# Attention and a bilinear feed-forward layer on one core: turned weights read in four transfers, maxima kept in PSUM, signs ahead of shifts, and half of the first queries at first

## The chip, the core and the metric

The kernel runs on one core of a Trainium2 chip. Its engines are TensorE (PE, with its own weight loads, PEld), VectorE (DVE), ScalarE (ACT), GpSimd (POOL) and SyncE (SP), which here only issues DMAs. The metric is the device time of one execution in microseconds (us); lower is better. Three executions of the kernel before took 1405.77, 1406.40 and 1414.82 us, so the median is 1406.40. A further execution was profiled.

## The reference

```python
# 8 batches x 8 heads, 576 positions, 64 columns a head; tau = 0.02
scores = scale * np.matmul(q, k.transpose(0, 1, 3, 2))
thresh = np.max(scores, axis=-1, keepdims=True) - tau
scores = np.where(scores >= thresh, scores, -1000000000.0)
scores = scores - np.max(scores, axis=-1, keepdims=True)
attn = np.exp(scores)
attn = attn / (np.sum(attn, axis=-1, keepdims=True) + 1e-09)
out = np.matmul(attn, v)
# the heads side by side: x is 4608 tokens x 512
a = x @ w_a          # 512 x 1536
b = x @ w_b          # 512 x 1536
return a * b @ w_out # 1536 x 512
```

Only scores within tau of the row's maximum count in the softmax. The weights w_a, w_b and w_out come as 64-bit numbers, and the kernel turns them into 32-bit ones by operations on their bits.

## The kernel before

**Units and slots.** Heads are taken in pairs (32 pairs, numbered i; four of them make a batch). The 576 queries of a pair are four tiles of 128 (u = 0 to 3) and a tail of 64; the tails of two pairs make one more tile (u = 4). One such tile is a unit. The main loop (L1117) takes one unit per slot g; the instructions are written out in the order of the loop, and each engine runs its own in that order. The first four pairs' units 0 and 1 come first (slots 0 to 7), then their units 2, 3 and 4.

**What a slot does.** `scores` (L389) multiplies queries by keys on PE into two PSUM tiles (one for each head), and takes the maximum of each head on DVE (L411) and from both the threshold (L412). `weigh` (L422) makes a bias from the maximum (ACT, L431), the exponential (ACT, L432) and the product of mask and exponential with its sum (DVE, L435), tile `tw`. Sums become reciprocals (L446, L448). Then the weights `tw` must be turned, so that PE can multiply them by the values (products `pv`, L546):
- units of slots 0 to 7 are turned on PE (L483, with the division by the sum folded into a diagonal matrix, L462), and copied out by ACT (L485) and DVE (L486);
- later units are divided on ACT (L454), turned in blocks of 32x32 on DVE (L502, `turn_blocks`), written to memory (`swap<-tw`) and read back block by block in the other order (`wT<-swap`, `turn_back`, L517).

The result `xT` is copied out of PSUM by DVE (L554) and ACT (L553). The feed-forward layer follows behind: its first products are `pab` (L854, and L750 with seven products in place of eight), its last ones `po` (L920). `advance` (L1024) puts portions of it between the steps of a slot.

**Queries and keys.** Those of the first four pairs are loaded as rows (`load_rows`, L193), transposed by PE (L378, twelve 96x96 blocks for 576 rows of both heads) and copied out of PSUM: queries on DVE (`prep_copy`, L383) into `first_sb`, keys on ACT. Those of the other pairs are loaded in another layout and transposed by DVE (L365, `prep`): their queries in two halves, `q0` for units 0 and 1, `q1` for the others.

**Weights, while they are converted.** They come in 36 pieces of 512 columns, in two 32-bit words a number. Slots 0 to 3 start two pieces each, slots 4 to 9 three, slots 10 to 14 two; each piece is finished a slot later. A piece takes ACT twice (upper word L298, lower word L299), POOL (clamp, L305), DVE (sign into the lower word, L311, which reads two tiles of SBUF; then a shift of the upper word by three bits, L319) and POOL again (add, L324). `convert_rest(g, k)` does sign, shift and add of the piece k: piece 0 behind the threshold of the slot, pieces 1 and 2 at the end of the slot, with a step of `advance` between them in slots 0 to 8. During slots 0 to 15 `state["wide"]` is true; the scores then take 128 columns of queries at a time.

**Queues.** All loads, and writes and reads of `swap`, go through SP. From slot 37 on (`state["paced"]`) `post` (L139) puts moves in a list, and `passed` (L169) takes them off as PE's work goes by, by their sizes; each waits for the PE instruction behind which it was taken off (L157). `flush` empties the list up to what a product needs. Before slot 37 moves are issued at once (L144).

Of the kernel before, what the change touches and what calls it, by code (L numbers as in the profile page):

```python
# [10 lines left out]
FP32 = mybir.dt.float32  # L11
# [43 lines left out]
def kernel(  # L55
# [38 lines left out]
    nc = tc.nc  # L94
    B, H, S, D = q.shape
    P = 128
# [3 lines left out]
    HP = H // 2  # L100
# [5 lines left out]
    R = 96  # L106
    NR = S // R
    SH = S // 2
    NF = DFF // P
    HALF = MAIN // 2  # L110
    GT = HALF // TAIL
    NSLOT = 9
    G = P // Q
# [4 lines left out]
    def pool(name, bufs, **kw):  # L118
        return ctx.enter_context(tc.tile_pool(name=name, bufs=bufs, **kw))
# [4 lines left out]
    small = pool("small", 2)  # L124
    scratch = pool("scratch", 5, space=bass.MemoryType.DRAM)
    psum = pool("psum", 4, space=PSUM)

    def banks(n, name):

        return psum.tile([P, 2, 512], FP32, tag="banks", name=name)[:, :, 0:n]  # L130
# [3 lines left out]
    NPR = len(pairs)  # L134
# [4 lines left out]
    def post(key, *moves):  # L139

        if not state["paced"]:
            for move in moves:
                state["turn"] += state["over"]
                (nc.scalar if state["turn"] % 2 else nc.sync).dma_start(*move)  # L144
        else:
            at = len(bulk)
            if key[0] in ("tw", "wT"):
                while at and bulk[at - 1][0][0] not in ("tw", "wT") and bulk[at - 1][1] >= state["slot"] - 1:
                    at -= 1
            bulk.insert(at, (key, state["slot"], moves))  # L150
# [13 lines left out]
    def flush(*keys):  # L164

        while any(key in keys for key, _, _ in bulk):
            pump(1, False)
# [25 lines left out]
    def load_rows(i, name, room, engine=nc.sync):  # L193

        b, hp = pairs[i]
        for j in range(2):
            rows = {"q": q, "k": k}[name][b, 2 * hp + j]
            engine.dma_start(room[:, :, j * D:(j + 1) * D], rows.rearrange("(n p) d -> p n d", p=R))
        loaded.setdefault(i, {})[name] = room

    def load_v(i, again=False):
# [24 lines left out]
    for f in range(NG):  # L226
        for c in range(HP):
            for dst, w in ((wa_sb, w_a), (wb_sb, w_b)):
                src = []
                for r in range(2):  # L230
                    chunks = [(2 * c + e) % HP * 2 + (r + (c >= HP // 2)) % 2 for e in range(2)]
                    cols = slice(f * CW + r * CH, f * CW + (r + 1) * CH)
                    rows = w[:, cols].bitcast(U32).rearrange("(k p) f -> p k f", p=D)
                    src.append(rows[:, chunks[0]:chunks[1] + 1:2])
                pieces.append((dst[:, f, 2 * c:2 * c + 2].rearrange("p k f -> p (k f)"), src))
    for F in range(NF):
# [3 lines left out]
    state = {"loaded": 0, "added": 0, "converted": 0, "rows": 0, "sums": False, "through": 0, "over": False,  # L240
             "layer": False, "paced": False, "all": False, "turn": 0, "due": NPIECES, "wide": True, "slot": 0, "reading": False, "first": 0}
# [8 lines left out]
    first_sb = first_u32.bitcast(FP32)  # L250
# [57 lines left out]
    def convert_sign(n):  # L308
        if n in stages:
            low, hi = stages[n].bitcast(U32), raws.pop(n)[:, :, 1]  # L310
            nc.vector.scalar_tensor_tensor(out=low, in0=hi, scalar=0x80000000, in1=low,  # L311
                                           op0=ALU.bitwise_and, op1=ALU.bitwise_or)
            if n in taken:
                extra.append(taken.pop(n))

    def convert_shift(n):
        if n in stages:
            top = pieces[n][0].bitcast(U32)
            nc.vector.tensor_scalar(top, top, 3, None, op0=ALU.logical_shift_left)  # L319

    def convert_add(n):
        if n in stages:
            top, low = pieces[n][0].bitcast(I32), stages.pop(n).bitcast(I32)
            nc.gpsimd.tensor_tensor(top, top, low, op=ALU.add)  # L324
            state["added"] += 1
# [6 lines left out]
    for _ in range(TW_BUFS):  # L332
        t = work.tile([P, 2 * NB, Q], FP32, tag="tw", bufs=TW_BUFS, name="rows")
# [21 lines left out]
    prepared, scored, weights, turned, whole = {}, {}, {}, {}, {}  # L355
# [5 lines left out]
    def prep(i, name):  # L361

        flush((name, i))
        mT = loaded[i].pop(name).rearrange("p n e -> p (n e)")
        nc.vector.transpose(mT, mT)  # L365
        prepared.setdefault(i, {})[name] = mT

    def prep_pe(i, name):

        m = loaded[i][name]  # L370
        if name == "q":
            mT = first_sb[:, i * S:(i + 1) * S]
        else:
            mT = work.tile([P, S], FP32, tag="kT", bufs=HP, name="kT")
        tp = banks(SH, "tp")
        for c in range(2):
            for n in range(NR // 2):
                nc.tensor.transpose(tp[:, c, n * R:(n + 1) * R], m[:, c * (NR // 2) + n], ident[0:R, 0:R])  # L378
        prepared.setdefault(i, {})[name] = mT
        return mT, tp  # L380

    def prep_copy(mT, tp):
        nc.vector.tensor_copy(mT.rearrange("p (c k) -> p c k", c=2), tp)  # L383

    def columns():

        return P if state["wide"] else D

    def scores(i, u):  # L389
        qT, kT = prepared[i]["q" if i < HP else "q1" if u > 1 else "q0"], prepared[i]["k"]  # L390
        base = HALF if i >= HP and u > 1 else 0
        sc = [banks(SH, "sc") for _ in range(2)]
        wide = D if u == NT else columns()
        each = [(c, t, j) for c in range(2) for t in range(2 if wide == D else 1) for j in range(2)]
        if units.index((i, u)) < BY_HEAD:
            each.sort(key=lambda x: x[2])
        for c, t, j in each:
            r = slice(j * D, (j + 1) * D)
            if u < NT:
                m, o, q0 = j, t, u * P + t * D - base  # L400
            else:
                m, o, q0 = t, j ^ t, MAIN - base
                qT, kT = prepared[i + t]["q" if i < HP else "q1"], prepared[i + t]["k"]
            nc.tensor.matmul(sc[m][o * D:o * D + wide, c], qT[r, q0:q0 + wide],  # L404
                             kT[r, c * SH:(c + 1) * SH], start=True, stop=True)
        mx = small.tile([P, 2], FP32, tag="mx", name="mx")
        thr = small.tile([P, 2], FP32, tag="thr", name="thr")
        bias = small.tile([P, 2], FP32, tag="bias", name="bias")
        for j in range(2):
            c = slice(j, j + 1)  # L410
            nc.vector.tensor_reduce(mx[:, c], sc[j], axis=AX.XY, op=ALU.max)  # L411
        nc.vector.tensor_scalar(thr, mx, cut, None, op0=ALU.subtract)  # L412
        scored[i, u] = (sc, thr, bias, mx)
# [53 lines left out]
    def turned_tile(here=None):  # L467
        if here == (0, NT):
            return sums_sb[:, NSUM - TURNED:].rearrange("p (g s e) -> p g s e", g=G + 1, s=NSLOT)
        return work.tile([P, G + 1, NSLOT, Q], FP32, tag="wT", bufs=2, name="wT")  # L470
# [46 lines left out]
    def turn_back(i, u):  # L517

        key = "wT", i, min(u // 2, 1) if i >= HP else u // 2
        if u < NT or i < HP:  # L520
            flush(("tw", i, u))
            swap = swaps.pop((i, u)).rearrange("g p e -> p g e")
            turned[i, u] = turned_tile((i, u))
            for y in range(0, G, 2):
                post(key, (turned[i, u][:, y:y + 2].rearrange("p g s e -> p g (s e)"), swap[:, y:y + 2]))
        if i >= HP and u == (3 if i % 2 else NT):
            flush(("tw", i - i % 2, NT))
            swap = swaps[i - i % 2, NT].rearrange("g p e -> p g e")
            for y in range(2):
                post(key, (turned[i, 2 + y][:, G].rearrange("p s e -> p (s e)"), swap[:, i % 2 * 2 + y]))  # L530
            if i % 2:
                del swaps[i - 1, NT]
# [561 lines left out]
    kT, tp = prep_pe(0, "k")  # L1094
# [7 lines left out]
    nc.vector.tensor_tensor(cut, cut, big, op=ALU.add)  # L1102
    early = {}

    def convert_rest(g, k):

        for n in early.get(g - 1, [])[k:k + 1]:
            convert_sign(n)
            convert_shift(n)
            convert_add(n)  # L1110

    n = 0
    for g in range(NPIECES):
# [3 lines left out]
    for g in range(len(units) + PV_LAG):  # L1117
# [9 lines left out]
        if BY_PE + 1 < g <= len(units) + 1:  # L1127
            n = g - PV_LAG
# [3 lines left out]
        if here:  # L1132
            i, u = units[g]
# [10 lines left out]
            running["owed"] -= NSLOT * P // 2  # L1144
        if g < 3:
            prep_copy(*prep_pe(g + 1, "q"))
        convert_rest(g, 0)
        if g == 0:
            for c in range(0, 2 * QUARTER - 2 * CW + 1, 2 * CW):
                extra.append(more_u32[:, c:c + 2 * CW].rearrange("p (f w) -> p f w", w=2))  # L1150
# [7 lines left out]
        load_weights(RAWS if g < 9 else 3, most=1)  # L1158
        if here:
            weigh(i, u)  # L1160
        for p in range(HP, NPR):
            for name, d in (("q0", 1), ("q1", 1)):
                if g == (second if name == "q1" else first)[p] - d - (name == "q1" and p % 2):
                    prep(p, name)
        if here and g < BY_PE:
            reciprocal(i, u, nc.vector)
        if g < 3:
            kT, tp = prep_pe(g + 1, "k")
# [3 lines left out]
        if g > BY_PE:  # L1172
            n = g - PV_LAG
# [25 lines left out]
        elif here:  # L1199
            reciprocal(i, u, nc.scalar if converting else nc.vector)  # L1200
            normalise(i, u)
        convert_rest(g, 1)
        if g <= BY_PE:
            advance(pace)
        convert_rest(g, 2)
        for n in early.get(g, [])[1:]:
            convert_first(n)
            convert_clamp(n)
        load_weights(RAWS if g < 9 else 3, most=1)
        for p in range(HP, NPR):  # L1210
            for name, d in (("q0", 3), ("k", 4), ("q1", 3)):
                if g == (second if name == "q1" else first)[p] - d - (name == "q1" and p % 2):
                    load(p, name)
        for p in range(1, NPR):
# [67 lines left out]
```

## Time and profile before

| | |
|---|---|
| runs | 1405.77, 1406.40, 1414.82 us |
| profiled execution | 1400.57 us, span 1398.8 us, mean granted clock 0.998 |
| PE busy | 1361.5 us (97%) |
| DVE busy | 1013.9 us (72%) |
| ACT busy | 680.8 us (49%) |
| POOL busy | 492.8 us (35%) |
| DMA | 223.21 MB in 327449 packets, mean 160 GB/s |

The page of the profile cuts the span into 40 slices of 35 us. Each digit below is the busy share of a slice in tenths (9 is 90% or more); the last row is what the DMA engines moved.

```profile
PE   7889999999999999999999999999999999999998
DVE  6999877787777768786767776778777776745425
ACT  6977555545554555544454545454545455431110
GB/s 211 241 212 223 204 206 173 174 170 187 174 154 168 190 192 155 176 190 160 143 143 160 186 180 159 136 190 169 181 130 161 199 190 154 137 146 19 4 19 18
```

The transfers that the change touches, by kind (written and read tile, queue, count, size, median time from issue to landing):

```profile
wT<-swap SPq DMA_DIRECT2D x242, 288.0 KB, 3.8
...
wT<-swap SPq DMA_DIRECT2D x56, 144.0 KB, 3.6
qT<-in_q_dram SPq DMA_DIRECT2D x112, 40.0 KB, 2.8
...
rows<-in_q_dram SPq DMA_DIRECT2D x4, 144.0 KB, 4.3
sums_u<-in_q_dram SPq DMA_DIRECT2D x4, 144.0 KB, 6.4
```

The maximum of slot 0 starts at 10.2 us, that of slot 5 at 46.0, of slot 10 at 93.7 and of slot 16, the first one without weights to convert, at 141.3 us. ACT's copies of weights, biases and exponentials stand almost back to back from 30 to 73 us: it idles under 4 us there. In slots 0 to 15 the threshold took, in this order, 0.23, 0.23, 0.65, 0.38, 0.61, 0.60, 0.58, 0.60, 0.59, 0.23, 0.26, 0.58, 0.27, 0.60, 0.48 and 0.60 us. Later, SP issues 1055 transfers between 350 and 1250 us; that takes it 553 us, 0.38 us for a read of turned weights, and it waits for PE's places for most of the rest.

### The profile page before, as it was taken

What the parts mean: (1) busy time and instruction counts of PE and PEld (TensorE: products, weight loads), DVE (VectorE), ACT (ScalarE), POOL (GpSimd) and SP (SyncE); (2) the same over time, 40 slices, a digit from 0 to 9 for tenths busy, and PEclk for the clock granted to TensorE, in tenths of its full rate; (3) what the DMA queues carried; (4) which work ended last, traced back from release to release, by engine and by line L of the source; (5) the groups of instructions that cost most, each with busy time, mean ns of one, the idle gap of its engine ahead of it and who ended that gap; (6) DMA issues with size and microseconds to landing.
All of it is one profiled execution on the core that took longest, in us unless ns stands there. A gap on an engine that the chain in (4) does not pass through costs nothing.

```text
span 1398.8 us, 76307 instructions
## 1 busy us (share of the span) xinstructions
PE 1361.5 (97%) x33836; PEld 1258.5 (90%) x33836; DVE 1013.9 (72%) x2205; ACT 680.8 (49%) x1248; POOL 492.8 (35%) x675
## 2 busy tenths in 40 slices
PE   7889999999999999999999999999999999999998
PEld 5677588999998799999999999998899998799998
DVE  6999877787777768786767776778777776745425
ACT  6977555545554555544454545454545455431110
POOL 2764543424150607060515142332515060708100
PEclk9999999999999999999999999999999999999999
DMA  9977876667666775676556775566656775550000
GB/s 211 241 212 223 204 206 173 174 170 187 174 154 168 190 192 155 176 190 160 143 143 160 186 180 159 136 190 169 181 130 161 199 190 154 137 146 19 4 19 18
DMA packets 327449, 223.21 MB, mean 160 GB/s; under 512 B 171600, under 2 KB 311632, under 8 KB 327120
## 3 DMA queue, kind: packets, MB, share of 16 engines
q1 hardware_dynamic: 323936, 216.95, 60.1%
q8 instruction: 266, 4.36, 1.3%
q10 hardware_dynamic: 3184, 1.38, 0.4%
q14 instruction: 63, 0.52, 0.1%
HBM read 128.58 MB, written 89.65 MB: 156 GB/s over the span
## 4 chain that ended last, share of the span: by engine, by line
PE 88%; DMA 5%; DVE 4%; SPq 2%; issue 1%; ACT 1%; ACTq 0%; DVEq 0%
PE pab L750 29%; PE po L920 22%; PE pab L854 18%; PE sc L404 9%; PE pv L546 9%; SPq L144 1%; DMA vm<-in_v_dram 1%; DMA wT<-swap 1%; DVE tw L435 1%; DVE mx L411 1%; DMA more_u<-in_moe_w_a_dram 1%; DVE low L311 0%; DMA more_u<-in_moe_w_b_dram 0%; DVE tw L502 0%; DMA sums_u<-in_k_dram 0%
## 5 line engine op out<-in xcount | busy, mean ns | idle before, releaser
L454 ACT ACTIVATE tw<-tw,rcp 128x576 f32<-128x576 f32 x272 | 196.1, 768 | 201.3 <-DVE rcp L448 201.3
L411 DVE TENSOR_REDUCE mx<-sc 128x1 f32<-128x576 f32 x288 | 204.6, 752 | 121.2 <-PE sc L404 120.9
L432 ACT ACTIVATE tw<-sc,bias,scalars 128x576 f32<-128x576 f32 x288 | 239.6, 832 | 10.4 <-DMA qT<-in_q_dram 0.4
L712 POOL TENSOR_TENSOR h<-h,u 128x512 f32<-128x512 f32 x28 | 35.2, 1277 | 590.4 <-DVE h L824 414.1
L435 DVE SCALAR_TENSOR_TENSOR tw<-sc,thr,tw 128x576 f32<-128x576 f32 x288 | 220.9, 797 | 12.3 <-ACT tw L432 11.9
L920 PE MATMUL po<-wo_sb,h 64*64 64x256 f32 (+1 forms) x3408 | 210.5, 367 | 0.0
L502 DVE STREAM_TRANSPOSE tw<-tw 128x576 f32<-128x576 f32 x272 | 194.4, 752 | 0.8 <-ACT tw L454 0.8
L920 PEld LDWEIGHTS po<-wo_sb,h 64*64 64x64 f32 x3408 | 169.8, 133 | 14.9
L404 PE MATMUL sc<-kT,qT 64*64 64x288 f32 x2016 | 170.3, 404 | 1.8 <-issue 0.9
L546 PE MATMUL pv<-wT,vm 64*64 64x128 f32 (+2 forms) x4896 | 164.0, 275 | 3.7 <-DMA vm<-in_v_dram 1.4
L546 PEld LDWEIGHTS pv<-wT,vm 64*64 64x64 f32 x4896 | 153.2, 133 | 12.0 <-issue 4.0
L920 PE MATMUL po<-sums_u,h 64*64 64x256 f32 x2448 | 156.6, 376 | 0.0
L883 POOL TENSOR_TENSOR h<-h 128x256 f32<-128x256 f32 x168 | 117.2, 731 | 110.9 <-PE po L920 106.1
L750 PE MATMUL pab<-xU,wb_sb 64*64 64x128 f32 x4352 | 137.8, 269 | 0.0
L920 PEld LDWEIGHTS po<-sums_u,h 64*64 64x64 f32 x2448 | 126.1, 133 | 12.3 <-DVE h L862 0.5
L750 PEld LDWEIGHTS pab<-xU,wb_sb 64*64 64x64 f32 x4352 | 133.3, 133 | 1.8 <-ACT h L806 0.5
L404 PEld LDWEIGHTS sc<-kT,qT 64*64 64x64 f32 x2016 | 108.8, 133 | 17.3 <-issue 4.9
L431 ACT ACTIVATE bias<-mx,scalars 128x1 f32<-128x1 f32 x288 | 82.7, 287 | 66.1 <-DVE mx L411 65.6
L553 ACT COPY xT<-pv 128x128 f32<-128x128 f32 (+1 forms) x68 | 17.6, 259 | 193.5 <-PE pv L546 193.5
L750 PE MATMUL pab<-xS,wa_sb 64*64 64x128 f32 x2176 | 108.5, 269 | 0.8 <-issue 0.8
L554 DVE COPY xT<-pv 64x128 f32<-64x128 f32 (+1 forms) x136 | 38.1, 280 | 80.5 <-PE pv L546 79.0
L535 ACT COPY kept<-po 128x512 f32<-128x512 f32 x65 | 34.8, 535 | 120.3 <-PE po L920 106.4
(163 smaller groups left out, 2468.7 us busy)
## 6 DMA issues: line engine op xcount, KB each, us to landing
wT<-swap SPq DMA_DIRECT2D x242, 288.0 KB, 3.8
swap<-tw SPq DMA_DIRECT2D x480, 144.0 KB, 3.1
vm<-in_v_dram SPq DMA_DIRECT2D x128, 72.0 KB, 2.6
swap<-tw SPq DMA_DIRECT2D x128, 72.0 KB, 2.9
kT<-in_k_dram SPq DMA_DIRECT2D x112, 72.0 KB, 3.2
wT<-swap SPq DMA_DIRECT2D x56, 144.0 KB, 3.6
out_dram<-kept SPq DMA_DIRECT2D x27, 256.0 KB, 3.7
qT<-in_q_dram SPq DMA_DIRECT2D x112, 40.0 KB, 2.8
```

The costliest lines, as they stand in the source:

```text
L404: nc.tensor.matmul(sc[m][o * D:o * D + wide, c], qT[r, q0:q0 + wide], kT[r, c * SH:(c + 1) * SH], start=True, stop=True)
L411: nc.vector.tensor_reduce(mx[:, c], sc[j], axis=AX.XY, op=ALU.max)
L431: nc.scalar.activation(bias[:, j:j + 1], mx[:, j:j + 1], AF.Copy, scale=e_nscale)
L432: nc.scalar.activation(wb[j], sb[j], AF.Exp, bias=bias[:, j:j + 1], scale=e_scale)
L435: nc.vector.scalar_tensor_tensor(out=wv, in0=sb[j], scalar=thr[:, j:j + 1], in1=wv, op0=ALU.is_ge, op1=ALU.mult, accum_out=sums[:, j:j + 1])
L454: nc.scalar.activation(w, w, AF.Copy, scale=rcp[:, j:j + 1])
L502: nc.vector.transpose(w, w)
L546: nc.tensor.matmul(pv[c * D:(c + 1) * D, y], vm[rows, s], wT[y](rows, s), start=(s == 0), stop=(s == NSLOT - 1))
L750: nc.tensor.matmul(out[c * D:(c + 1) * D, r, f * P:(f + 1) * P], w[g][k][rows, w0:w0 + D], moving[k][rows], start=(fresh and k == 0 and f ...
L854: nc.tensor.matmul(pab[c:c + columns(), r], w[rows, f // n, k, fs + c:fs + c + columns()], moving, start=(k == 0), stop=(k == H - 1))
L883: (nc.vector if state["over"] else nc.gpsimd).tensor_tensor(*a, **kw)
L920: nc.tensor.matmul(po[c * D:(c + 1) * D, r, y, cut], ht[rows, t0:t0 + D], other[rows, f, cut], start=(f == 0), stop=(f == NF // 2 - 1))
```

## The change

Four edits:
1. The queries of the first four pairs are loaded, transposed and copied only up to row 288 (units 0 and 1 need 256). For units 2, 3 and 4 their second half comes as `q1`, as with the other pairs: 16 loads of 40 KB, and four transposes on DVE.
2. While weights are converted, the two maxima go to two free columns of the first head's PSUM tile, next to its scores, and not to a small tile in SBUF.
3. For the second and third piece of a slot, both signs come before both shifts and adds.
4. From slot 37 on, a unit's turned weights are read in four transfers of 144 KB in place of two of 288 KB.

```diff
     def load_rows(i, name, room, engine=nc.sync):
+        n = NR // 2 if name == "q" else NR
         for j in range(2):
-            rows = {"q": q, "k": k}[name][b, 2 * hp + j]
-            engine.dma_start(room[:, :, j * D:(j + 1) * D], rows.rearrange("(n p) d -> p n d", p=R))
+            rows = {"q": q, "k": k}[name][b, 2 * hp + j, 0:n * R]
+            engine.dma_start(room[:, 0:n, j * D:(j + 1) * D], rows.rearrange("(n p) d -> p n d", p=R))
...
-            mT = first_sb[:, i * S:(i + 1) * S]
+            mT = first_sb[:, i * SH:(i + 1) * SH]
...
-        for c in range(2):
+        for c in range(1 if name == "q" else 2):
             for n in range(NR // 2):
                 nc.tensor.transpose(tp[:, c, n * R:(n + 1) * R], m[:, c * (NR // 2) + n], ident[0:R, 0:R])
...
-        qT, kT = prepared[i]["q" if i < HP else "q1" if u > 1 else "q0"], prepared[i]["k"]
+        qT, kT = prepared[i]["q1" if u > 1 else "q" if i < HP else "q0"], prepared[i]["k"]
...
-        sc = [banks(SH, "sc") for _ in range(2)]
+        whole_sc = [psum.tile([P, 2, 512], FP32, tag="banks", name="sc") for _ in range(2)]
+        sc = [x[:, :, 0:SH] for x in whole_sc]
...
-        mx = small.tile([P, 2], FP32, tag="mx", name="mx")
+        if state["wide"]:
+            mx = whole_sc[0][:, 0, SH:SH + 2]
+        else:
+            mx = small.tile([P, 2], FP32, tag="mx", name="mx")
...
-            for y in range(0, G, 2):
-                post(key, (turned[i, u][:, y:y + 2].rearrange("p g s e -> p g (s e)"), swap[:, y:y + 2]))
+            n = 1 if state["paced"] else 2
+            for y in range(0, G, n):
+                post(key, (turned[i, u][:, y:y + n].rearrange("p g s e -> p g (s e)"), swap[:, y:y + n]))
...
-        for n in early.get(g - 1, [])[k:k + 1]:
-            convert_sign(n)
-            convert_shift(n)
-            convert_add(n)
+        for step in steps:
+            for n in early.get(g - 1, [])[k]:
+                step(n)
...
-        convert_rest(g, 0)
+        convert_rest(g, slice(0, 1))
...
-        for p in range(HP, NPR):
-            for name, d in (("q0", 1), ("q1", 1)):
+        for p in range(NPR):
+            for name, d in (("q0", 1), ("q1", 1))[p < HP:]:
...
-        convert_rest(g, 1)
+        convert_rest(g, slice(1, 3), (convert_sign,))
         if g <= BY_PE:
             advance(pace)
-        convert_rest(g, 2)
+        convert_rest(g, slice(1, 3), (convert_shift, convert_add))
```

In the program that this gives, PE's instructions stand in the same order but for the twelve transposes less and the other source of the queries.

More of the change, by code (lines that the diff above doesn't have):

```diff
@@ L382, in prep_copy @@
     def prep_copy(mT, tp):
-        nc.vector.tensor_copy(mT.rearrange("p (c k) -> p c k", c=2), tp)
+        nc.vector.tensor_copy(mT, tp[:, 0])
     def columns():
@@ L389, in scores @@
     def scores(i, u):
-        qT, kT = prepared[i]["q" if i < HP else "q1" if u > 1 else "q0"], prepared[i]["k"]
-        base = HALF if i >= HP and u > 1 else 0
-        sc = [banks(SH, "sc") for _ in range(2)]
+        qT, kT = prepared[i]["q1" if u > 1 else "q" if i < HP else "q0"], prepared[i]["k"]
+        base = HALF if u > 1 else 0
+        whole_sc = [psum.tile([P, 2, 512], FP32, tag="banks", name="sc") for _ in range(2)]
+        sc = [x[:, :, 0:SH] for x in whole_sc]
         wide = D if u == NT else columns()
@@ L402, in scores @@
                 m, o, q0 = t, j ^ t, MAIN - base
-                qT, kT = prepared[i + t]["q" if i < HP else "q1"], prepared[i + t]["k"]
+                qT, kT = prepared[i + t]["q1"], prepared[i + t]["k"]
             nc.tensor.matmul(sc[m][o * D:o * D + wide, c], qT[r, q0:q0 + wide],
                              kT[r, c * SH:(c + 1) * SH], start=True, stop=True)
-        mx = small.tile([P, 2], FP32, tag="mx", name="mx")
+        if state["wide"]:
+            mx = whole_sc[0][:, 0, SH:SH + 2]
+        else:
+            mx = small.tile([P, 2], FP32, tag="mx", name="mx")
         thr = small.tile([P, 2], FP32, tag="thr", name="thr")
@@ L1103, with convert_rest @@
     early = {}
-    def convert_rest(g, k):
-        for n in early.get(g - 1, [])[k:k + 1]:
-            convert_sign(n)
-            convert_shift(n)
-            convert_add(n)
+    def convert_rest(g, k, steps=(convert_sign, convert_shift, convert_add)):
+        for step in steps:
+            for n in early.get(g - 1, [])[k]:
+                step(n)
     n = 0
@@ L1209 @@
         load_weights(RAWS if g < 9 else 3, most=1)
-        for p in range(HP, NPR):
-            for name, d in (("q0", 3), ("k", 4), ("q1", 3)):
+        for p in range(NPR):
+            for name, d in (("q0", 3), ("k", 4), ("q1", 3))[2 * (p < HP):]:
                 if g == (second if name == "q1" else first)[p] - d - (name == "q1" and p % 2):
```

## The prediction

> **What bounds the kernel now.** I read the table of windows first: busy microseconds of each engine in each stretch of the profiled execution (columns: stretch, length, PE, PEld, DVE, ACT, POOL, granted clock, DMA share, GB/s).
>
> ```profile
> 0.00:35.00 35.00, 25.39 (x314) 20.31 (x316) 21.39 (x55) 21.38 (x43) 10.13 (x19) 1.00 1.11 211
> 35.00:70.00 35.00, 28.13 (x596) 24.19 (x594) 33.90 (x76) 31.53 (x67) 27.20 (x32) 1.00 1.07 241
> 70.00:105.00 35.00, 30.29 (x532) 27.14 (x530) 33.17 (x66) 27.87 (x57) 24.27 (x26) 0.95 0.74 212
> 105.00:140.00 35.00, 32.51 (x484) 27.85 (x484) 34.04 (x77) 27.02 (x55) 16.23 (x17) 1.00 0.79 223
> ...
> 350.00:700.00 350.00, 348.50 (x8913) 324.96 (x8909) 263.39 (x582) 174.75 (x316) 117.83 (x178) 1.00 0.65 170
> ```
>
> PE has 1.5 us of idle time in the 350 us of the last row: it is the bound there. Its idle time lies in the first 140 us, while weights are converted: 9.6 + 6.9 + 4.7 + 2.5 = 23.7 us. From 35 to 140 us DVE is the fullest engine (101.1 of 105 us), with ACT behind it. Whatever the change gains comes out of these 23.7 us.
>
> Second, the waits of 35 to 105 us (engine, line, releaser: us in total, times, longest), of which these are PE's on DVE:
>
> ```profile
> PE pab L854 <- DVE tw L435: 5.9, 5, 1.6
> ...
> PE tp L483 <- DVE xT L554: 3.2, 2, 2.2
> ```
>
> Third, the timeline of DVE, then of POOL, in slot 7 (start, duration):
>
> ```profile
> 70.47 0.83 DVE L311 SCALAR_TENSOR_TENSOR low<-more_u,low 128x512 uint32<-128x512 uint32 x1
> ...
> 71.88 1.66 DVE L311 SCALAR_TENSOR_TENSOR low<-raw,low 128x512 uint32<-128x512 uint32 x1
> 73.47 0.41 DVE L319 TENSOR_SCALAR wa_sb<-wa_sb 128x512 uint32<-128x512 uint32 x1
> ...
> 75.25 0.59 DVE L412 TENSOR_SCALAR thr<-mx,scalars 128x2 f32<-128x2 f32 x1
> ...
> 80.97 1.49 DVE L319 TENSOR_SCALAR wb_sb<-wb_sb 128x512 uint32<-128x512 uint32 x1
> ```
>
> ```profile
> 71.72 1.28 POOL L324 TENSOR_TENSOR wb_sb<-wb_sb,low 128x512 int32<-128x512 int32 x1 [0.96 <-DVE wb_sb L319]
> 73.96 1.27 POOL L324 TENSOR_TENSOR wa_sb<-wa_sb,low 128x512 int32<-128x512 int32 x1 [0.96 <-DVE wa_sb L319]
> 75.20 0.61 POOL L305 TENSOR_SCALAR wa_sb<-wa_sb 128x512 f32<-128x512 f32 x1
> ...
> 80.54 1.64 POOL L324 TENSOR_TENSOR wa_sb<-wa_sb,low 128x512 int32<-128x512 int32 x1 [0.96 <-DVE wa_sb L319]
> ```
>
> A DVE step on SBUF that starts beside a POOL step ends when that one ends: a shift of 0.41 us takes 1.49, a sign of 0.68 takes 1.66, and the threshold (256 numbers, 0.23 us alone) takes 0.59. The mean over 35 to 140 us shows it again, while a copy out of PSUM is steady (0.22 us also at 57.83 us, beside POOL):
>
> ```profile
> L319 DVE TENSOR_SCALAR wb_sb<-wb_sb 128x512 uint32<-128x512 uint32 x10 | 7.8, 777 | 0.0
> L412 DVE TENSOR_SCALAR thr<-mx,scalars 128x2 f32<-128x2 f32 x12 | 6.0, 499 | 0.4
> ...
> L554 DVE COPY xT<-pv 64x64 f32<-64x64 f32 x12 | 2.7, 222 | 0.3
> ```
>
> **288 queries at first.** Eight loads of 144 KB become 72 KB: 590 KB less, 2.8 us at the 211 GB/s of the first row. The first pair loses 3 PE transposes at 0.12 to 0.18 us (0.5 us), and its copy on DVE goes from 128x576 (0.755 us) to 128x288; between that row and 128x128 (0.273 us) this is 0.445 us, so 0.3 us. Both lie on the path to the first scores: -0.8 us. The other nine transposes fall where PE waits: nothing. Loads of weights come up to 2.8 us earlier; what waits for them is ACT's 0.7 us at 47 us and 1.4 us of PE on values, so between 0 and -2.1 us; since ACT is full behind it I take half, -1.0. The missing half of the queries comes later: 16 loads of 40 KB behind slots 5, 7, 10 and 12 (1.8 us of SP each time, behind the weights then posted), and four DVE transposes 128x320 of 0.505 us in slots 7, 9, 12 and 14, behind the masked exponentials: +2.0 us on a full DVE, charged below. The first of these loads lands at 66 to 68 us by the 2.8 us of its kind; DVE wants it at 67 to 70 us.
>
> **Maxima in PSUM.** The 16 thresholds of slots 0 to 15 took 7.5 us; unstretched they take 16 x 0.23 = 3.7. DVE saves 3.8 us, nearly all in slots with POOL work. But the maxima share a bank with the scores, and the built program waits by bank: ACT's first bias (L431) now waits for the threshold, where before it waited for the first maximum; the second maximum waits for the first; and DVE's first masked exponential (L435) waits for the second bias. The trace has no such wait; from its rows, the bias starts 0.75 (second maximum) + 0.23 + some 0.1 later. In slot 0, where the chain has nothing beside it, that is +1.1 us. In slots 1 to 8 ACT (bias, exponential, bias: 0.29 + 0.83 + 0.29 = 1.4 us) runs beside DVE work of 0.46 + 0.7 + 0.4 = 1.5 us: hidden by 0.1 us. From slot 9 on the two block transposes of L502 (1.5 us of DVE) lie there too: hidden. The second maximum, which ran back to back, costs 0.12 us more by the gaps between dependent DVE steps: 16 x 0.12 = 1.9 us of DVE.
> [...]
>
> **Signs ahead of shifts.** In slots 5 to 10, which convert three pieces, one step of DVE per slot is stretched by the POOL add before it: 54.35 (1.50), 63.38 (1.49), 71.88 (1.66), 80.97 (1.49), 91.92 (1.51), 101.40 (1.51): about 6 x 1.07 = 6.4 us. With both signs first, the first add starts with the second shift. Then two adds and two clamps (2 x 1.28 + 2 x 0.61 = 3.8 us on POOL) run beside the next slot's maxima, threshold and first sign. Maxima and PSUM reads cover 1.5 + 0.2 + 0.46 = 2.2 us; the rest can meet that sign: 0.3 to 0.9 us back per slot, taken as 0.5. Slots with two pieces keep their order.
>
> **Four transfers.** From slot 37 on 288 KB reads become two of 144 KB: the same bytes and descriptors, 194 more issues of 0.38 us on SP. From 350 to 1250 us SP issues for 553 us of 900; this adds some 65. Every read waits for its own place on PE, and the last one of four is posted about 8 PE instructions later, under 1 us. It lands in 3.6 us (row of 144 KB) rather than 3.8. Between the last landing and the product that reads it there is a median of 5.45 us (70 groups; smallest 1.0, 1.36, 2.55), and PE has 1.5 us to win in 350. Nothing either way; up to +1 where the smallest margins go.
> [...]
>
> **Sum**, against the profiled execution (span 1398.8, 1400.6 with what lies around it):
> - start and slot 0: -0.8 + 1.1 = +0.3
> - earlier weights and values: -1.0
> - slots 1 to 4: thresholds -0.6, second maxima +0.5: 0
> - slots 5 and 6: -2.1 (stretch) - 0.8 (thresholds) + 1.0 (clash later) + 0.2 = -1.7 on DVE; PE's wait for xT (2.2 us) lies right behind, so most counts: -1.3
> - slots 7 to 10: -4.3 - 1.1 + 2.0 + 0.5 + 1.0 (two transposes) = -1.9 on DVE; some of it ends in ACT's place: -1.5
> - slots 11 to 15: -1.4 + 0.6 + 1.0: 0
> - the four transfers: 0
>
> Together -3.5 us: 1397.1 on the profiled run. That run was 5.8 us below the median of the runs shown (1405.77, 1406.40, 1414.82), so I set the sum against the median: about **1403 us**.
>
> **Rivals.**
> 1. All of the stretch is won: 6.4 + 3.8 us of DVE, and PE never rests at 74 to 78 us, after which 16 products took 2.08 us rather than 1.09 and the granted clock of the row is 0.95 (5% of 35 us: 1.75 us). With 1.0 for the transfers and less the 1.9 us of second maxima and 2.0 of transposes, -9: 1397. Against it: ACT's 31.5 of 35 us. Chance 0.15.
> 2. Slower by the bank waits: ACT's biases stand behind the threshold in every slot, and ACT, which idles under 4 us from 30 to 73 us, has weight pieces queued behind them. It decides as soon as ACT's spare time before the bias is under 0.9 us, as in most of slots 2 to 8. Price: 1.1 in slot 0, up to 0.9 in seven slots, 1.9 for second maxima, 2.0 for transposes, less half of what is won (5): +6, 1412. For it: the margin of 0.1 us above. Chance 0.2.
> 3. Slower by the split: turned weights come 3 us later than now, because SP is late by several issues. Then only the groups with less margin pay (2.0 + 1.6 + 0.5: +4, 1410); to lose 14 us the lateness would have to exceed the median 5.45 us. Chance 0.1.
> 4. The stretch only changes its victim: the signs meet the adds as the shifts did (71.88 is a sign), the next sign takes the rest; with the extra transposes 0 to +2: 1406 to 1408. Chance 0.15.
> [...]
>
> The forecast (a gain of 1 to 6 us) has 0.4. From the -9 of rival 1 and the +6 of rival 2, with 3 us of scatter in the median (one run of three lies 8 us out), the range is 1392 to 1414. About 1% (14 us) can be told from no change here: faster than that (under 1392) 0.08, from rival 1 and a lucky median; slower (over 1420) 0.1, from rivals 2 and 3 at several times their price; the same 0.82.
>
> **What would show it.** Thresholds at 0.23 us beside POOL; signs and shifts of slots 5 to 10 at 0.68 and 0.41 but for the first sign of the next slot; the wait of products on xT under 1 us; slot 16's first maximum, now at 141.3 us, at 137 to 139; from 350 us on, PE's idle time as before and its waits on turned weights near nothing. The prediction is wrong if slot 16 starts later than 141.3 us, if ACT's bias becomes the releaser of DVE and PE in slots 2 to 8, or if 350 to 1250 us changes by over 2 us.

## The result, and the profile after

The changed kernel takes 1417.38 us (median of 8 executions, 1411.83 to 1422.34); the kernel before took 1407.38 us (8 executions, 1403.06 to 1414.82) beside it. The ratio is 1.0061, with a 95% interval of 1.0038 to 1.0084: the change makes the kernel 0.6% slower, some 9 us. The profiled execution has a span of 1415.5 us, against 1398.8 before; these two lie further apart than the medians, because the profiled execution of the kernel before was a quick one (1400.57 us for a median of 1407.38).

The table of windows of the changed kernel (stretch, length, busy time of PE, PEld, DVE, ACT, POOL, clock, DMA share, GB/s):

```profile
0.00:35.00 35.00, 24.03 (x320) 18.71 (x320) 22.11 (x57) 22.37 (x45) 12.19 (x21) 1.00 1.10 207
35.00:70.00 35.00, 28.90 (x597) 24.72 (x599) 31.37 (x78) 31.11 (x68) 26.43 (x31) 1.00 1.08 232
70.00:105.00 35.00, 29.94 (x528) 26.75 (x526) 32.03 (x69) 28.42 (x57) 25.12 (x27) 0.95 0.83 220
105.00:140.00 35.00, 32.54 (x478) 27.30 (x479) 32.84 (x75) 25.84 (x53) 14.64 (x16) 1.00 0.86 237
...
350.00:700.00 350.00, 347.45 (x8848) 325.84 (x8843) 262.30 (x578) 174.80 (x316) 114.11 (x172) 1.00 0.67 172
700.00:1050.00 350.00, 343.19 (x8971) 318.38 (x8966) 249.81 (x549) 167.86 (x302) 109.12 (x163) 1.00 0.63 163
1050.00:1250.00 200.00, 195.76 (x4917) 178.37 (x4912) 146.43 (x326) 100.08 (x181) 72.97 (x111) 0.99 0.62 160
```

While weights are converted, DVE is less busy than before (96.2 us for 101.1 from 35 to 140 us), and PE's idle time there is about what it was: 13.6 us for 14.1. The loss lies where the prediction saw nothing at stake. From 350 to 1250 us PE idles 13.6 us; before it was 4.1, by the row of 350 to 700 us shown above (PE busy 348.50 us) and these two of the kernel before:

```profile
700.00:1050.00 350.00, 348.78 (x9078) 334.43 (x9072) 255.01 (x559) 171.63 (x308) 111.85 (x166) 1.00 0.63 163
1050.00:1250.00 200.00, 198.63 (x5140) 183.63 (x5132) 143.80 (x319) 99.20 (x178) 66.39 (x102) 1.00 0.64 169
```

Set against the kernel before, the starts of the slots' first maxima show four jumps there (times of the changed kernel): at about 477 us (+2.2 us), 820 us (+3.7), 963 us (+2.4) and 1124 us (+3.9). Between the jumps the two kernels keep step to within 1 us.

The waits of DVE from 350 to 1250 us name what is late (engine, line, releaser: us in total, times, longest). First the kernel before, then the changed one:

```profile
DVE kT L365 <- DMA kT<-in_k_dram: 2.1, 4, 0.8
...
DVE qT L365 <- DMA qT<-in_q_dram: 0.3, 1, 0.3
```

```profile
DVE kT L366 <- DMA kT<-in_k_dram: 19.4, 8, 4.3
...
DVE qT L366 <- DMA qT<-in_q_dram: 3.6, 6, 0.9
```

It is the keys, and not the turned weights: loads of K, four of 72 KB a pair, which DVE has to transpose in its place in the order of the program. SP's timeline ahead of the second jump shows how they come to be late (start, duration; what lies between the issues of a row, a wait for a place on PE too, is in its duration):

```profile
799.52 3.38 SPq L157 DMA_DIRECT2D swap<-tw  x4
802.99 4.91 SPq L157 DMA_DIRECT2D wT<-swap  x8
808.02 3.63 SPq L157 DMA_DIRECT2D swap<-tw  x4
811.74 2.68 SPq L157 DMA_DIRECT2D kT<-in_k_dram  x4
814.51 2.67 SPq L157 DMA_DIRECT2D qT<-in_q_dram  x4
```

The same place in the kernel before:

```profile
794.37 2.01 SPq L157 DMA_DIRECT2D swap<-tw  x4
796.47 3.64 SPq L157 DMA_DIRECT2D wT<-swap  x4
800.21 2.01 SPq L157 DMA_DIRECT2D swap<-tw  x4
802.33 3.33 SPq L157 DMA_DIRECT2D kT<-in_k_dram  x4
```

In both, hardly a pause lies between SP's issues (0.5 us at most). K starts 12.2 us behind the first write of `swap` and not 8.0. Of these 4.2 us the eight reads in place of four make only 1.3 (4.91 us for 3.64); the other 3.0 are in the writes, of which one in each row took over 1.9 us to issue (1.92 and 1.95). So it is not these reads alone, but that SP has no time left to catch up. Over 350 to 1250 us its pauses of more than 0.3 us add up to 252 us in the kernel before and to 133 us in the changed one, and the longest stretch without one grows from 25 to 49 us. The transfers of K are no slower: from issue to landing they take 3.24 us at the median before and 3.11 after. What follows, on DVE and then on PE in the changed kernel:

```profile
811.73 1.28 DVE L826 TENSOR_TENSOR u<-u,pab 128x512 f32<-128x512 f32 x2
817.34 0.78 DVE L366 STREAM_TRANSPOSE kT<-kT 128x576 f32<-128x576 f32 x1 [4.33 <-DMA kT<-in_k_dram]
818.14 0.59 DVE L560 COPY xT<-pv 64x128 f32<-64x128 f32 x2
```

```profile
815.04 0.64 PE L406 MATMUL sc<-kT,qT 64*64 64x288 f32 x2
818.87 0.95 PE L406 MATMUL sc<-kT,qT 64*64 64x288 f32 x11 [3.19 <-DVE xT L560]
```

DVE stands 4.33 us before the transpose, the copy of `xT` that is queued behind it frees its PSUM tile late, and PE, which needs that tile for scores, stands 3.19 us. PE's wait is put down to `xT`; one has to go on to what DVE waited for to find the load.

All transfers of turned weights, from the page:

```profile
wT<-swap SPq DMA_DIRECT2D x444, 144.0 KB, 3.1
wT<-swap SPq DMA_DIRECT2D x48, 288.0 KB, 4.0
```

Halves land in 3.1 us rather than 3.8, but that is time which nothing waited for. SP issues 1232 transfers in 664 us from 350 to 1250 us, where it was 1055 in 553 us.

### The profile page after: what moved, and what is told of

Read it like the earlier page. It is cut to its first block, busy times and chain, and to the rows that moved or that the text cites. A ratio compares the mean times of both kernels' runs of the same rounds, so it can differ in the third digit from the quotient of the medians.

```text
span 1415.5 us, 76770 instructions
## 1 busy us (share of the span) xinstructions
PE 1365.3 (96%) x33824; PEld 1244.2 (88%) x33824; DVE 1009.1 (71%) x2209; ACT 678.9 (48%) x1248; POOL 493.4 (35%) x675
## 4 chain that ended last, share of the span: by engine, by line
PE 86%; DMA 6%; DVE 4%; SPq 2%; issue 1%; POOL 0%; ACT 0%; DVEq 0%; POOLq 0%; ACTq 0%
PE pab L756 30%; PE po L926 21%; PE pab L860 16%; PE sc L406 9%; PE pv L552 9%; SPq L144 2%; DMA raw<-in_moe_w_a_dram 1%; DMA wT<-swap 1%; DMA swap<-tw 1%; DMA kT<-in_k_dram 1%; DVE sc L416 1%; DMA sums_u<-in_moe_w_a_dram 1%; DVE tw L507 1%; DMA raw<-in_moe_w_b_dram 1%; DMA qT<-in_q_dram 0%
## 5 line engine op out<-in xcount | busy, mean ns | idle before, releaser
L416 DVE TENSOR_REDUCE mx<-sc 128x1 f32<-128x576 f32 x256 | 181.8, 751 | 110.3 <-PE sc L406 109.8
L406 PE MATMUL sc<-kT,qT 64*64 64x288 f32 (+1 forms) x2128 | 187.8, 406 | 12.7 <-DVE xT L560 3.3
L926 PEld LDWEIGHTS po<-wo_sb,h 64*64 64x64 f32 x3408 | 166.2, 133 | 20.6 <-issue 1.5
L552 PEld LDWEIGHTS pv<-wT,vm 64*64 64x64 f32 x4896 | 153.9, 133 | 13.6 <-issue 4.9
L406 PEld LDWEIGHTS sc<-kT,qT 64*64 64x64 f32 (+1 forms) x2128 | 116.5, 135 | 35.6 <-issue 15.0
L926 PEld LDWEIGHTS po<-sums_u,h 64*64 64x64 f32 x2448 | 122.8, 133 | 16.2 <-DVE h L868 0.9
L559 ACT COPY xT<-pv 128x128 f32<-128x128 f32 (+1 forms) x68 | 17.7, 260 | 196.7 <-PE pv L552 196.7
L436 ACT ACTIVATE bias<-mx,scalars 128x1 f32<-128x1 f32 x256 | 73.5, 287 | 57.1 <-DVE mx L416 57.1
L756 PE MATMUL pab<-xT,wa_sb 64*64 64x128 f32 x1856 | 92.5, 269 | 0.4 <-DVE kept L542 0.4
```

The lines of the kernel that those rows point to most:

```text
L436: nc.scalar.activation(bias[:, j:j + 1], mx[:, j:j + 1], AF.Copy, scale=e_nscale)
L552: nc.tensor.matmul(pv[c * D:(c + 1) * D, y], vm[rows, s], wT[y](rows, s), start=(s == 0), stop=(s == NSLOT - 1))
L756: nc.tensor.matmul(out[c * D:(c + 1) * D, r, f * P:(f + 1) * P], w[g][k][rows, w0:w0 + D], moving[k][rows], start=(fresh and k == 0 and f ...
L926: nc.tensor.matmul(po[c * D:(c + 1) * D, r, y, cut], ht[rows, t0:t0 + D], other[rows, f, cut], start=(f == 0), stop=(f == NF // 2 - 1))
```

## The experiments

Each kernel was timed beside the kernel before on the same chip; all ratios are to it. The levels of the kernel before differ by some us from chip to chip and from one session to the next (1402 to 1410), so only ratios are compared.

**Without the split, and the split alone.** The first is the changed kernel with this undone, the second the kernel before with only this done:

```diff
-            for y in range(0, G, 2):
-                post(key, (turned[i, u][:, y:y + 2]..., swap[:, y:y + 2]))
+            n = 1 if state["paced"] else 2
+            for y in range(0, G, n):
+                post(key, (turned[i, u][:, y:y + n]..., swap[:, y:y + n]))
```

> The changed kernel, but turned weights are read in two transfers throughout, as before the change. Theory (SP's queue): the four-way split costs SP some 110 us of issuing from 350 to 1250 us, so loads of K land late and DVE waits for them (21 us in the changed kernel, 2 us before it); without the split these waits are 2 to 5 us again, PE idles 4 to 6 us from 350 to 1250 us, and the ratio to before is 0.997 to 1.001. Rival (the loss is made while weights are converted, by the maxima in PSUM or the later queries): the ratio stays above 1.004.

> The kernel before, with the four-way split alone. Theory (SP's queue): DVE waits 15 to 22 us for K from 350 to 1250 us, PE idles 11 to 15 us there, the ratio is 1.005 to 1.008. Rival (the loss is made while weights are converted): 0.999 to 1.002.

Without the split: 0.9997 (0.9983 to 1.0010), no wait of DVE for K or queries of 0.3 us or more from 350 to 1250 us. The split alone: 1.0070 (1.0052 to 1.0089), and in the waits of DVE

```profile
DVE kT L365 <- DMA kT<-in_k_dram: 16.1, 7, 3.5
```

with 12.4 us of idle time on PE from 350 to 1250 us. The whole loss is the split's; the other three edits together neither win nor lose anything that can be measured. A gain of 3.5 us, as forecast, would be 0.9975, which lies outside the interval.

**Issues or places on PE.** In the changed kernel two reads of 144 KB are taken off the list together, so that only the first waits for a place on PE:

```diff
-            for y in range(0, G, n):
-                post(key, (turned[i, u][:, y:y + n]..., swap[:, y:y + n]))
+            for y in range(0, G, 2):
+                post(key, *[(turned[i, u][:, z:z + n]..., swap[:, z:z + n])
+                            for z in range(y, y + 2, n)])
```

> The changed kernel with four reads, but two of them are taken off the list together, so that places on PE to wait for are as many as before the change and only the issues are doubled. Theory (SP's own time for an issue): K is as late as in the changed kernel, ratio 1.004 to 1.007. Rival (the places on PE, each of which holds SP up): K comes in time, ratio 0.997 to 1.001.

1.0051 (1.0033 to 1.0069), DVE waits 12.5 us for K. Most of the loss stays with the places as they were: the places are not its main cause.

**Issues without smaller reads.** In the kernel before, behind each read of 288 KB:

```diff
                 post(key, (turned[i, u][:, y:y + 2]..., swap[:, y:y + 2]))
+                if state["paced"]:
+                    spare = small.tile([P, 2], FP32, tag="spare", name="spare")
+                    post(key, (spare[0:1], v[0, 0, y:y + 1, 0:2]))
```

> The kernel before, two reads of 288 KB as they were, and from slot 37 on behind each of them a read of 8 bytes into a tile that nothing uses: as many issues on SP as with the split, without smaller reads. Theory (SP's time for an issue): K late, DVE waits 12 to 22 us for it from 350 to 1250 us, ratio 1.004 to 1.008. Rival (it is the reads in four parts that are late): no waits, ratio 0.999 to 1.002.

1.0052 (1.0035 to 1.0069), and DVE's waits are

```profile
DVE kT L365 <- DMA kT<-in_k_dram: 13.7, 5, 4.0
```

The 180 spare issues from 350 to 1250 us take SP 47 us, 0.25 us at the median (a read of turned weights takes 0.38). Moving no data to speak of, they cost about three quarters of what the split alone does. The spare reads have places on PE of their own, but the run before this one rules out the places. So it is the number of issues, not the size of a read, that makes K late. One more way in which many transfers could hold SP up can be read from the traces: the 1711 transfers that SP and ACT issue in the changed kernel report their ends on eight semaphores in turn, and of the 1703 that follow another on the same semaphore none starts before that one has landed (before: none of 1493). On SP these waits are 1.5 us from 350 to 1250 us before and none in the changed kernel.

**K a slot earlier.** In the changed kernel the loads of K are listed five slots ahead in place of four; first throughout, then only from slot 37 on (`4 + state["paced"]`).

> The changed kernel with four reads, but the loads of K are put on the list one slot (some 8 us) earlier. Theory (late K is what the split costs): DVE's waits for K fall from 21 us to under 4, PE's idle time from 350 to 1250 us from 13.6 us to 4 to 6, ratio 0.996 to 1.000. Rival (the smaller reads themselves are what is late, and K only the one seen): turned weights or queries are waited for instead, ratio 1.003 to 1.007.

> The changed kernel with four reads, and the loads of K a slot earlier only from slot 37 on. Loading K earlier from the start made slots 16 to 20 some 3 us later; that should be gone. Theory: no waits for K, ratio 0.997 to 1.000, no better than two reads (0.9997), since the smaller reads win nothing. Rival (the four reads do win something once K is in time): ratio under 0.997.

Throughout: 1.0016 (1.0000 to 1.0031). From slot 37 on: 1.0033 (1.0015 to 1.0051). In both DVE's waits for K are gone, but PE still idles 7.5 and 9.5 us from 350 to 1250 us (13.6 in the changed kernel, 4.1 before), and both expectations of the ratio were missed. Against 1.0061, late K is half to three quarters of what the split costs; only the first ratio's interval still touches 1. With K moved ahead on the same queue, turned weights come late in its place. PE's waits from 350 to 1250 us in the second kernel:

```profile
PE pv L552 <- DMA swap<-tw: 3.0, 2, 2.3
PE pv L552 <- DVE tw L440: 1.9, 2, 1.6
...
PE pv L552 <- DMA wT<-swap: 0.5, 1, 0.5
```

There, 8 of 45 groups of products begin less than 1 us behind the landing of their last turned weights; in the kernel before, none of 46 do. This fits a queue that is short of time, where the order decides only who waits. That the first of the two comes out lower than the second was not expected either; their intervals overlap. Nor did slot 16 start earlier with K early only from slot 37 on (140.7 us for 141.1), as the reason given for that run would have it.

**K issued by ACT.** From slot 37 on, in the changed kernel:

```diff
+            if name == "k" and state["paced"]:
+                for move in moves:
+                    nc.scalar.dma_start(*move)
+                continue
```

> The changed kernel with four reads, but from slot 37 on the loads of K are issued by ACT, which has half its time free there, and not by SP. Theory (SP's queue): K is early, SP issues some 55 us less from 350 to 1250 us, DVE's waits for K are gone, ratio 0.996 to 1.000 although the reads stay split in four. Rival (the small reads themselves cost): ratio 1.003 to 1.007.

1.022 (1.0186 to 1.0254): both theories missed. The edit also takes K's places on PE away: ACT issues a load where it stands in ACT's order. SP issues for 559 us, as before the change, and DVE waits neither for K nor for queries. But the loads stand ahead of the next bias in ACT's order, and the bias starts 0.05 us behind the end of the last issue. ACT's timeline at 458 us (ACTq is what it issues):

```profile
459.27 0.76 ACT L463 ACTIVATE tw<-tw,rcp 128x576 f32<-128x576 f32 x1
459.88 3.42 ACTq L191 DMA_DIRECT2D kT<-in_k_dram  x2
463.35 0.29 ACT L440 ACTIVATE bias<-mx,scalars 128x1 f32<-128x1 f32 x1 [3.32 <-DMA kT<-in_k_dram]
```

ACT is busy for 48% of the span, but it is not free here: bias and exponential are awaited by DVE, and PE idles 19.5 us from 350 to 1250 us. The 3.42 us are one issue of 1.18 us, a gap of 1.64 us and one of 0.59 us. The trace settles the gap: the last load uses the semaphore of the pair's first load, which lands at 462.69 us; the issue follows at 462.71. Of the 26 gaps of over 0.2 us between loads of a pair on ACT, 25 end 0.02 us behind the landing of the transfer that used the semaphore last. So what follows these loads on ACT waits for earlier transfers to land.

**The other three edits, one at a time.** The maxima in PSUM, signs ahead of shifts, and 288 queries at first, each alone in the kernel before, and the last two together.

> The kernel before, with the maxima in PSUM alone. As predicted: thresholds 0.23 us throughout (3.8 us of DVE won), the first bias behind the threshold (slot 0 1.1 us later), second maxima 0.12 us later each; slot 16's first maximum at 140 to 142 us (141.3 before), ratio 0.998 to 1.001. Rival (the wait of ACT's bias for the threshold decides): slot 16 at 143 us or later, ratio 1.001 to 1.004.

> The kernel before, with signs ahead of shifts alone. As predicted: the stretched shift or sign of slots 5 to 10 is gone (6 x 1.07 us), half of it given back by the next slot's first sign; slot 16's first maximum at 137 to 139.5 us. Rival (the clash only moves): 140.5 to 142 us. In both cases SP, which is nearly full from slot 16 to 22, takes part of it back: slot 24's first maximum, 198.6 us before, at 197 to 199 us, ratio 0.998 to 1.000.

> The kernel before, with 288 queries at first alone. As predicted: slot 0's first maximum 0.8 us earlier (9.4 for 10.2), slot 5's 1 to 2 us earlier. What the queries that come later cost: 16 more issues on SP and 2 us of DVE up to slot 14; slot 16's first maximum at 140 to 142 us, slot 24's at 198 to 200 us, ratio 0.999 to 1.002.

> The kernel before, with signs ahead of shifts and 288 queries at first, without the maxima in PSUM and the split. If slots 0 to 5 lose 1.6 us by the waits of the maxima in PSUM, slot 5's first maximum stands at 42.5 to 43.5 us (46.0 before, 43.2 to 45.0 with the maxima in PSUM too), slot 16's at 137 to 139, ratio 0.996 to 0.999. If the gain is lost in slots 11 to 24 anyway: slot 24 at 197 to 199 us, ratio 0.999 to 1.001.

Ratios, the start of some slots' first maxima, and how much longer than unstretched the DVE steps of slots 0 to 15 took (16 thresholds over 0.23 us, 36 shifts over 0.41, 36 signs over 0.68; all us):

| kernel | ratio | slot 0 | slot 5 | slot 11 | slot 16 | slot 24 | thresholds, shifts, signs |
|---|---|---|---|---|---|---|---|
| before | | 10.2 | 46.0 | 102.8 | 141.3 | 198.6 | 3.8, 7.6, 1.8 |
| maxima in PSUM | 0.9995 (0.9981 to 1.0009) | 10.4 | 45.7 | 102.8 | 141.3 | 199.8 | 0.0, 7.5, 1.9 |
| signs first | 0.9983 (0.9968 to 0.9999) | 10.6 | 46.5 | 102.3 | 141.6 | 200.8 | 4.8, 2.4, 2.0 |
| 288 queries | 1.0000 (0.9985 to 1.0014) | 9.2 | 42.8 | 99.6 | 139.1 | 197.0 | 3.7, 7.7, 1.3 |
| signs, 288 queries | 0.9999 (0.9985 to 1.0013) | 9.5 | 44.2 | 98.7 | 138.7 | 196.8 | 5.8, 2.2, 2.1 |
| all but the split | 0.9997 (0.9983 to 1.0010) | 9.0 | 45.0 | 98.5 | 138.8 | 197.8 | 0.0, 3.4, 2.2 |
| changed | 1.0061 (1.0038 to 1.0084) | 9.5 | 44.7 | 99.6 | 140.5 | 200.4 | 0.0, 3.1, 2.5 |

Up to slot 36 the last two rows are the same program, and so are three of the experiments above; over these five executions slot 16 ranges from 138.5 to 140.7 us and slot 24 from 196.7 to 200.8. So a row tells about 2 us from nothing, not less. Each edit does its work on DVE, and DVE's saving does not arrive: with the maxima in PSUM, and with signs first, slot 16 stands where it stood; for the signs this is what the rival said (140.5 to 142 us), not the theory (137 to 139.5). The 288 queries bring some 3 us by slot 5, more than the 1 to 2 expected, and keep 2 of them to slot 16. By slot 24 little is left of anything, and no ratio but that of the signs alone differs from 1, and that one barely; among this many ratios, one such is weak evidence. Whether its 0.2% comes from these slots stays open, for its profile shows no slot from 0 to 24 that gains 1 us to stay. Nor does slot 5 show the price of the maxima in PSUM that the last expectation looked for: 44.2 us without them, 43.2 to 45.0 with them.

**One read of 576 KB, the opposite of the split.** With signs first, as the best of the single edits:

> The kernel before with signs ahead of shifts, and the opposite of the split: from slot 37 on turned weights are read in one transfer of 576 KB. SP issues some 45 us less from 350 to 1250 us. Theory (SP's queue): no waits for K at all, PE's idle time from 350 to 1250 us 2 to 4 us, ratio 0.996 to 0.999. Rival (a read that starts only when all of its data is there and lands as one comes too late for its product): PE waits for turned weights for 5 us or more, ratio 1.001 to 1.006.

1.0035 (1.0020 to 1.0050); both missed. SP issues for 515 us, and waits for K stay small (2.7 us). Turned weights are not late: no group of products begins less than 1 us behind its last landing. PE's idle time from 350 to 1250 us is 9.6 us, and the profile puts most of it to nothing it can see:

```profile
PE pab L751 <- issue: 6.6, 12, 1.0
PE pv L547 <- issue: 2.0, 3, 0.8
```

The profile's releasers do not tell what PE stood for, but its DMA packets do. All 15 of these gaps end 1.0 to 1.6 us behind the landing of a packet of 16 KB on queue q8, which the page marks as "instruction" (266 packets; one lands about every 4.8 us, so that a moment picked at random has a chance of 0.13 to lie there). The packets keep step with PE: in the kernel before it starts 256 instructions at the median from one landing to the next (from 350 to 1250 us; half of the counts lie from 216 to 294). PE most likely stood for its own instructions. Before, 6 such gaps take 3.0 us; here they take 8.6 us, and the difference of 5.6 us is about the 0.35% that the run lost. Why the instructions come late more often here stays open. Only the signs alone come out below the kernel before, and barely; the changed kernel without its split is as fast as the kernel before.

## Why the prediction was wrong

Forecast was 1403 us, a gain of 3.5 us, with a range of 1392 to 1414; measured were 1417.38 us and a loss of 0.4 to 0.8%. Two steps failed, one of them alone decides the sign. That the loss stayed within the 14 us that the prediction called the same (chance 0.82) was luck: it came from a term that the prediction had put at nothing. One of its own signs of being wrong appeared: from 350 to 1250 us PE's idle time grew by 9.5 us, where it allowed 2.

- **The step that failed: "Nothing either way; up to +1" for the four transfers.** It checked SP's mean occupancy (553 + 65 of 900 us) and the margin of the turned weights themselves, median 5.45 us. It did not ask who is queued behind them on SP. In the trace of before, the last load of K lands less than 1 us ahead of its transpose for 8 of the 28 pairs that DVE transposes, and `post` (L147 to L149) lists writes of `swap` and reads of turned weights ahead of other loads of the same slot or the one before, so that it is K that added reads push back. The 65 us were too small as well: they are the median issue of 0.38 us times the added reads, but about one issue in ten takes more than 1 us, the mean is 0.52 us before and 0.54 us after, and the issuing grew by 111 us for 177 more issues. That took half of SP's pauses (252 to 133 us). The term is about +10 us (split alone 1.0070; 7 to 12 by its interval), not 0.
- **Rival 3** had the right engine and the wrong victim: it let turned weights be late, and its price (+4 us) came from their margins. But for one wait of 0.7 us beside the spare reads, PE waits for its victim only when K is put ahead of them (8 groups of products under 1 us). With the split as it is, 3 of 45 groups come under 1 us in the changed kernel and 5 of 45 with the split alone, and PE waits for none of them.
- **The size of a read: no gain on either side.** Four reads of 144 KB gave 1.0070 alone, by way of what is queued behind them. One read of 576 KB, with signs first, gave 1.0035.
- **Thresholds: right.** DVE by line and shape, 35 to 140 us, of the changed kernel:

```profile
L320 DVE TENSOR_SCALAR wb_sb<-wb_sb 128x512 uint32<-128x512 uint32 x10 | 5.9, 592 | 0.0
...
L560 DVE COPY xT<-pv 64x64 f32<-64x64 f32 x12 | 2.7, 222 | 0.3
L417 DVE TENSOR_SCALAR thr<-sc,scalars 128x2 f32<-128x2 f32 x12 | 2.6, 220 | 0.4
```

  0.499 us became 0.220, also beside POOL; 3.8 us were won on DVE as counted. Unstretched it took 0.23 us from SBUF.
- **The bias behind the threshold: right.** In slot 0, the changed kernel, DVE and then ACT:

```profile
9.48 1.64 DVE L416 TENSOR_REDUCE sc<-sc 128x1 f32<-128x576 f32 x2 [2.67 <-PE sc L406]
11.15 0.22 DVE L417 TENSOR_SCALAR thr<-sc,scalars 128x2 f32<-128x2 f32 x1
```

```profile
11.47 0.26 ACT L436 ACTIVATE bias<-sc,scalars 128x1 f32<-128x1 f32 x1 [4.37 <-DVE thr L417]
```

  The same in the kernel before:

```profile
10.24 1.42 DVE L411 TENSOR_REDUCE mx<-sc 128x1 f32<-128x576 f32 x2 [2.59 <-PE sc L404]
```

```profile
11.04 0.29 ACT L431 ACTIVATE bias<-mx,scalars 128x1 f32<-128x1 f32 x1 [3.17 <-DVE mx L411]
```

  The bias starts 1.99 us behind the first maximum; before it was 0.80. That is +1.2 us for the +1.1 predicted. That the wait goes by bank was the author's reading of the program; the trace names the threshold. The two maxima take 1.64 us for 1.42: 0.22 us more, not 0.12. Rival 2, in which this wait decides (+6 us), did not come true: the maxima in PSUM alone gave 0.9995.
- **288 queries: the start was right**, slot 0 0.76 us earlier for 0.8. By slot 5 it is 1 to 3 us, as estimated with the earlier weights. From slot 11 to 16 the time grew where the sum had 0: 40.0 us for 38.5 with signs and queries, 39.5 with queries alone. That the later queries are the reason is not shown, since signs alone took 39.3 and a row tells no less than 2 us.
- **Signs first: the stretch went as said** (shifts 7.6 to 2.4 us of excess), and the signs took little of it (1.8 to 2.0). Slot 7 of the changed kernel, on DVE:

```profile
69.02 1.06 DVE L312 SCALAR_TENSOR_TENSOR low<-more_u,low 128x512 uint32<-128x512 uint32 x1
70.01 0.68 DVE L312 SCALAR_TENSOR_TENSOR low<-raw,low 128x512 uint32<-128x512 uint32 x1
...
70.94 0.41 DVE L320 TENSOR_SCALAR wb_sb<-wb_sb 128x512 uint32<-128x512 uint32 x1
71.28 0.41 DVE L320 TENSOR_SCALAR wa_sb<-wa_sb 128x512 uint32<-128x512 uint32 x1
```

  Where the maxima stayed in SBUF, it was the thresholds that the later adds met: 4.8 and 5.8 us of excess for 3.8. Rival 4 rightly looked for a new victim, but named the signs. The split of the thresholds' 3.8 us over the slots was a little off in the sum: by their row, slots 1 to 4 hold 0.95 us and not 0.6, slots 7 to 10 hold 0.76 and not 1.1.
- **The sum of the first three, -3.5 us, failed in its last step**: from DVE's saving to the time. By slot 16 the profiles without further change show 0.6 to 2.8 us of gain; by slot 24 -2.2 to +1.9, around nothing; timed, 0.9997. From 35 to 140 us DVE's own waits for PE's scores grew from 1.4 to 3.9 us and for ACT's sums from 0.4 to 1.8, and PE's waits for DVE fell only from 11.9 to 10.1 us, while one for POOL's copy of `xT` (1.8 us) was new: PE idles 13.6 us there for 14.1. From 140 to 200 us it idles 5.2 us for 2.5 (4.1 without the split). What bounds the slots there stays open. In the chain of waits from 95 to 200 us, SP's issues hold 13.8% before and 20.5% after, but over the five executions of that same program they range from 8.5 to 24.7%.

## What to carry to other kernels

Before splitting a transfer, count the issues against the queue and look at every transfer that stands behind it: find the loads with the least margin between landing and use, whatever tile they fill. Price an issue by the mean and not by the median (0.54 us for 0.38 here). Here a queue that issued for 61% of the time (553 of 900 us) went 25 us without a pause of 0.3 us, and the 180 issues of 8 bytes added to it, 47 us, gave 1.0052. Ask of time freed on the fullest engine whether the wait that ends last is on that engine: here 3.8 us less of thresholds on DVE gave 0.9995, with slot 16 at 141.3 us as before.

## What the runs showed of the hardware

- An issue's price on SP did not go by its bytes: at the median 0.25 us for 8 bytes in one row, 0.38 us for 144 as for 288 KB, 0.58 us for 72 KB of K. Of 1232 issues in the changed kernel 130 took more than 1 us and made 192 of the 664 us; of the 180 reads of 8 bytes none did.
- A DVE step on SBUF stretched beside POOL, a threshold of 256 numbers, took 0.50 us in the mean; the same step reading PSUM took 0.22 beside the same POOL work. The prediction read that a stretched step ends when POOL's ends. Its six rows show it a little later: the five shifts end 0.28 to 0.29 us behind the POOL add, the sign 0.55 us.
